# One tile shape for the products of attention and a long convolution on one core: eight tiles of 64 rows and 32 columns into two banks, one score tile a turn

## The chip, the cores and the metric

The kernel runs on one core of a Trainium2 chip, as one program. The metric is device microseconds from start to end, lower is better. Times of the kernel before are given from three runs, and one further execution was profiled; the profile's lines are of that execution.

## The reference

Two computations that share nothing but the output, whose halves they fill:

```python
def _A_ref(x, wq, wk, wv, wo):           # x: 1 x 2048 x 512, 32 heads of 16, one shared k and v
    q = (x @ wq).reshape(B, S, H, Dh).transpose(0, 2, 1, 3)
    k = x @ wk
    v = x @ wv
    p = softmax(einsum("bhqd,bkd->bhqk", q, k) * (Dh ** -0.5))
    o = einsum("bhqk,bkd->bhqd", p, v)
    return o.transpose(0, 2, 1, 3).reshape(B, S, H * Dh) @ wo

def _B_ref(q, k, v, shift_k, ssm_k, ssm_D):   # 1 x 2048 x 512
    # k_shift: causal convolution of 4 taps along S, per channel
    kv = k_shift * v
    y = irfft(rfft(kv, 2 * S) * rfft(ssm_k, 2 * S))[:S]   # causal convolution over all of S, per channel
    return q * (y + kv * ssm_D)

out = concatenate([_A_ref(...), _B_ref(...)], axis=-1)
```

## The kernel before

**Attention.** The 2048 queries of 32 heads form 32 groups of 4 heads times 512 queries (`NQ` = 32), and the keys 16 blocks of 128 (`NKT` = 16). A *score tile* is one key block for two heads, 128 keys by 2 x 512 queries; there are 2 x 32 x 16 = 1024 of them. For each, `scores` (L784) makes two matmuls side by side, one head in array rows 0 to 48 and one in rows 64 to 112 (each number split into f16 parts, 49 rows with the shift), into the two PSUM banks of a buffer `s`; ScalarE takes the exponential of both banks at once into a buffer `p` (L792). `pv` (L821, for the last group L806) then multiplies `p` by `vx` (v and a column of ones, 32 columns, f32) and adds over the key blocks into a sum: four column tiles of 128 rows by 32 columns side by side, 256 columns a step, one step for each score tile. After 32 steps VectorE copies the sum to `ao` (L831), and SyncE stores it.

**The other work** is cut into generators, called threads: the query projections (`rest_of_q`), the division of finished heads (`wo_heads`), the output projection (`wo_part`), and the convolution as a transform of 2048 = 128 x 16 points: matmuls with tables for the 128 (`forward`, `backward`), VectorE for the 16 (`dft4`, `dft16`, `product`) and the short convolution (`conv_short`). Their matmuls go through `mm` (L203): four column tiles of 128 rows by 32 columns. Transposes (L305) and the bounds of the queries (L638) have other shapes.

**The order** is written out by the program itself, and each engine works its own instructions strictly in this order. `attend` makes turns of three score tiles: three times `scores`, then `pv` steps, and around them what `_Fill` hands out of the threads. `_Fill` holds a credit of TensorE units and one of VectorE nanoseconds; both grow each turn by `RATE`, up to `MOST`. A thread yields what its next piece costs; `WHOLE` pieces are made at once, `PARTS` may be split. `hurry` puts a thread first when its due step comes near.

**PSUM** has eight banks: three score buffers of two banks (`ps`), and two single banks (`pf`), which the sum of `pv` and the products of the threads share in turn. SBUF holds seven buffers `p` (`PB`).

Of the kernel before, what the change touches and what calls it, by code (L numbers as in the profile page):

```python
# [19 lines left out]
P = 128  # L20
# [7 lines left out]
KR = 49  # L28
# [19 lines left out]

RATE = 3.0, 2500.0
EASY = 2  # L50
MOST = 4.0, 2900.0
# [41 lines left out]
WHOLE, PARTS = 0, 1  # L93


class _Emit:
    def __init__(self, ctx, tc, I, out):
        self.ctx, self.tc, self.nc, self.I, self.out = ctx, tc, tc.nc, I, out
        e = ctx.enter_context
        self.c = e(tc.tile_pool(name="c", bufs=1))  # L100
        self.ps = e(tc.tile_pool(name="ps", bufs=3, space=PSUM))
        self.pf = e(tc.tile_pool(name="pf", bufs=2, space=PSUM))
        self.w = e(tc.tile_pool(name="w", bufs=2))
        self.dr = e(tc.tile_pool(name="dr", bufs=1, space=DRAM))
        self.n = 0
        self.step = 0
        self.seen = set()

# [4 lines left out]
    def bank(self):  # L113
        return self.pf.tile([P, 512], F32, tag="f", name=self.nm("f"))
# [90 lines left out]
    def columns(self, bank, first, w, x, last=False, dve=0):  # L205

        n, k = 0, x.shape[-1] // P
        while n < k:  # L210
            g = yield k - n, dve, CONT if bank else NEW, PARTS
            start = not bank
            if start:
                bank.append(self.bank())
            c = slice(P * n, P * (n + g))
            n += g
            self.mm(bank[0][:, P * first + c.start : P * first + c.stop], w, x[:, c], start, last and n == k)
# [5 lines left out]
    def products(self, bank, pairs, last=False, dve=0):  # L223

        n, k = 0, len(pairs)
        while n < k:
            g = yield k - n, dve, CONT if bank else NEW, PARTS
            start = not bank
            if start:
                bank.append(self.bank())  # L230
            for w, x in pairs[n : n + g]:
                n += 1
                self.mm(bank[0], w, x, start, last and n == k)
                start = False
# [15 lines left out]
    def forward(self, src, c, m, ft):  # L250

        b = []
        for q in range(2):
            yield from self.columns(b, 2 * q, ft[:, q, :], src, q == 1, 700 * q)
        self.nc.vector.tensor_copy(c[:, :, m, :], b[0].rearrange("p (q n) -> p q n", q=2))  # L255
# [9 lines left out]
    def conv_load(self):  # L265
# [6 lines left out]
        yield 1, 600, NEW, WHOLE  # L272
        tp = self.bank()
        for ct in range(4):
            nc.tensor.transpose(tp[0:4, ct * P : (ct + 1) * P], sk[:, ct, :], self.ident)
        tps = w.tile([4, 512], F32, tag="s2", bufs=S2, name="tps")
        nc.vector.tensor_copy(tps, tp[0:4, :])
# [14 lines left out]
    def long_forward(self, blk, hin, ch):  # L292
# [8 lines left out]
        def turn(m):  # L301
            b = self.bank()
            for i in range(2):
                for ct in range(2):
                    nc.tensor.transpose(b[:, (2 * i + ct) * P : (2 * i + ct + 1) * P], hv[:, ct, m + i], self.ident)  # L305
            hT[m] = self.s2("hT")
            nc.vector.tensor_copy(hT[m], b.rearrange("p (i n) -> p i n", i=2))

        for m in (0, 2):
            yield 2, 700, NEW, WHOLE  # L310
            turn(m)
        for m in range(0, 16, 2):
            if m < 12:
                ft[m // 2 + 2] = self.table("ff", m // 2 + 2)
                yield 2, 700, NEW, WHOLE
                turn(m + 4)
# [80 lines left out]
    def backward(self, blk, cx, places):  # L397
# [15 lines left out]
        for m2 in range(8):  # L413
# [5 lines left out]
            b = []  # L419
            for i in range(2):  # L420
                m = 2 * m2 + i
                for cc in range(2):
                    x = cx[:, cc, 4 * g2[m // 4] + g1[m % 4], :]
                    last = i == cc == 1
                    yield from self.columns(b, 2 * i, ft[m2][:, i, cc, :], x, last, 700 * last)
            nc.vector.tensor_tensor(r, b[0].rearrange("p (i n) -> p i n", i=2), q[m2], ALU.mult)  # L426
# [93 lines left out]
    def x_turn(self, c):  # L520

        nc = self.nc
        b = [self.wide() for _ in range(2)]
# [18 lines left out]
    def kv(self):  # L542

        b = self.bank()
# [36 lines left out]
    def v_turn(self, kv):  # L581

        nc = self.nc
        b = self.bank()
# [6 lines left out]
    def k_max(self, kv):  # L591
# [6 lines left out]
        b = self.bank()  # L598
# [16 lines left out]
    def q_out(self, g, c, b, spread=False):  # L615
# [3 lines left out]
        nc.vector.tensor_scalar(cut, b, LIM, -LIM, ALU.min, ALU.max)  # L619
# [33 lines left out]
    def prologue(self):  # L653
# [15 lines left out]
        b = self.bank()  # L669
# [3 lines left out]
        self.x_turn(1)  # L673
        for dk in range(4):
# [10 lines left out]
        b = self.bank()  # L685
        cut = [self.k_cut(0, rows[0])]
        self.bound(0, 0, b, st)
        b1 = self.bank()
# [13 lines left out]
        self.scores(2)  # L702
# [8 lines left out]
    def rest_of_q(self):  # L711
# [5 lines left out]
        for c in range(4):  # L717
            for g in range(4):
# [3 lines left out]
                if c or g > 1:  # L722
                    b = []
                    for dk in range(4):
                        pairs = self.three(self.wq[g][:, :, dk, :], self.xT[c][:, :, dk, :])
                        yield from self.products(b, pairs, dk == 3, 2600 * (dk == 3))
                    self.q_out(g, c, b[0])
                yield WAIT, 2
                yield 2, 1100, NEW, WHOLE
                self.bound(g, c, self.bank())  # L730
# [21 lines left out]
    def flag(self):  # L752
# [10 lines left out]
        yield 1, 200, NEW, WHOLE  # L763
        b = self.bank()
# [5 lines left out]
    def scores(self, u):  # L770
# [11 lines left out]
        for e in range(2):  # L782
            rows = slice(64 * e, 64 * e + KR)
            self.nc.tensor.matmul(  # L784
                s[:, e, :],
                self.kst[rows, k * P : (k + 1) * P],
                part(rows),
                start=True,
                stop=True,
            )  # L790
# [4 lines left out]
    def pv(self, x):  # L795

# [4 lines left out]
        if n == NQ - 1:  # L801
            h, k = divmod(x % (2 * NKT), NKT)
            if k == 0:
                self.acc = self.bank()
            for j in range(4):
                nc.tensor.matmul(  # L806
                    self.acc[32 * j : 32 * j + 32, 0:256],
                    self.vx[:, k, :],
# [431 lines left out]
```

## Time and profile before

| | us |
|---|---|
| three runs | 1046.73 (median), 1045.3 to 1048.16 |
| the profiled execution | 1045.31 |
| its span | 1043.5 |
| VectorE's copies of sums (31) | 21.4 |
| DMA, mean over the span | 84 GB/s |
| granted TensorE clock, mean | 0.996 |

The span runs from the first to the last instruction in the profile; the execution's time has a little around it. A group of the profile gives a line, an engine, an operation and tiles, then the count, the busy time, the mean duration of one in ns, and the idle time of the engine just before them with what ended it. A matmul's duration holds the way through the array, so several overlap: the distance between starts says what one costs in a row of them. PEld is TensorE's loading of weights, which runs beside matmuls. An f32 matmul stands in the profile as two instructions with one weight load each; in the lists of the order below it is one row, and its loads aren't shown. A timeline's row gives start, length and a count of like instructions that follow each other, and in brackets the idle time ahead with its cause.

### The profile page before, as it was taken

The numbers are of one execution on the slowest core, as the hardware profiler recorded it, in microseconds if no ns is written. First come the engines' busy times: TensorE is split into PE (matmuls) and PEld (weight loads), VectorE is DVE, ScalarE is ACT, GpSimd is POOL, SyncE is SP. The second block draws the span as 40 slices with busy tenths as digits, with TensorE's granted clock in tenths as the row PEclk, the third lists the DMA queues.
The fourth block names the chain that finished last, engine by engine and source line by source line (L and its number), as shares of the span: only waits on it lengthen the run. The fifth ranks groups of instructions, "written<-read, shape, count | busy, mean of one in ns | idle before, by whom it ended". The sixth has DMA issues, their size and how long they took to land.

```text
span 1043.5 us, 31945 instructions
## 1 busy us (share of the span) xinstructions
PE 990.4 (95%) x14019; PEld 449.3 (43%) x14019; DVE 654.4 (63%) x881; ACT 972.4 (93%) x1039; POOL 105.0 (10%) x158
## 2 busy tenths in 40 slices
PE   6899999999999999999999999999999899999986
PEld 4344444444433334444444444444444334444432
DVE  4736873877497887776861578378888990211133
ACT  4699989999999999999999999999999999999994
POOL 4131301000000000030101312000000000121000
PEclk9999999999999999999999999999999999999999
DMA  7335524112211211031314534101032101331101
GB/s 243 128 97 181 190 77 167 45 51 82 91 56 45 75 35 40 22 122 57 96 56 132 183 123 149 42 20 44 33 97 71 52 29 40 109 121 45 51 2 44
DMA packets 47549, 87.30 MB, mean 84 GB/s; under 512 B 11132, under 2 KB 26026, under 8 KB 46380
## 3 DMA queue, kind: packets, MB, share of 16 engines
q1 hardware_dynamic: 33996, 43.50, 12.9%
q0 software_dynamic: 11648, 40.89, 12.1%
q8 instruction: 111, 1.82, 0.7%
q10 hardware_dynamic: 1760, 0.81, 0.3%
q14 instruction: 34, 0.28, 0.1%
HBM read 60.16 MB, written 25.02 MB: 82 GB/s over the span
## 4 chain that ended last, share of the span: by engine, by line
PE 70%; ACT 15%; DVE 8%; issue 6%; DMA 1%; ACTq 0%; SPq 0%
PE f L821 32%; PE s L784 22%; ACT p L792 14%; PE f L203 14%; DVE sp L141 2%; DVE ao L831 1%; PE f L305 1%; PE f L806 1%; DMA wqf<-in_A_wq 1%; DVE xT L540 1%; PE x L203 0%; ACT xT L539 0%; DVE sp L395 0%; DVE sp L255 0%; DVE t L362 0%
## 5 line engine op out<-in xcount | busy, mean ns | idle before, releaser
L792 ACT ACTIVATE p<-s 128x1024 f32<-128x1024 f32 x1024 | 960.1, 1037 | 41.5 <-PE s L784 35.9
L821 PE MATMUL f<-p,vx 128*32 128x256 f32 x7936 | 494.7, 381 | 8.1 <-DVE ao L831 8.1
L784 PE MATMUL s<-st,kst 49*128 49x512 f16 x2048 | 317.6, 380 | 19.1 <-ACT p L792 16.4
L821 PEld LDWEIGHTS f<-p,vx 128*32 128x32 f32 x7936 | 235.1, 110 | 196.9 <-issue 33.6
L784 PEld LDWEIGHTS <-kst 49*128 49x128 f16 x2048 | 100.1, 94 | 253.3 <-issue 206.5
L141 DVE TENSOR_TENSOR sp<-sp 128x1024 f32<-128x1024 f32 x96 | 111.5, 1213 | 0.0
L255 DVE COPY sp<-f 128x512 f32<-128x512 f32 x64 | 44.1, 689 | 63.6 <-PE f L203 62.5
L831 DVE COPY ao<-f 128x512 f32<-128x512 f32 x31 | 21.4, 691 | 71.4 <-PE f L821 71.4
L203 PE MATMUL f<-xT,wq 128*32 128x512 f16 x768 | 58.8, 391 | 0.1
L141 DVE TENSOR_TENSOR sp<-sp,sp 128x1024 f32<-128x1024 f32 x48 | 56.3, 1216 | 0.2
L203 PE MATMUL f<-wo,o 128*32 128x512 f16 x720 | 54.4, 383 | 0.0
L426 DVE TENSOR_TENSOR r<-f,q 128x512 f32<-128x512 f32 x16 | 11.0, 688 | 63.0 <-PE f L203 63.0
L259 POOL DMA_DIRECT2D ff<-in_ff x32 | 17.5, 548 | 266.7 <-PE f L203 266.7
L203 PE MATMUL f<-a,ff 128*32 128x256 f32 (+1 forms) x648 | 38.8, 338 | 1.6 <-DVE sp L255 1.6
L203 PE MATMUL f<-hT,ff 128*32 128x256 f32 (+1 forms) x648 | 38.8, 338 | 0.0
L203 PE MATMUL f<-sp,fi 128*32 128x256 f32 (+1 forms) x680 | 38.3, 331 | 0.0
L427 POOL DMA_DIRECT2D out<-r x16 | 11.5, 717 | 250.1 <-DVE rl L879 147.0
L364 DVE TENSOR_TENSOR a<-a,t 128x512 f32<-128x512 f32 x48 | 33.2, 691 | 1.5
L362 DVE TENSOR_TENSOR t<-kk,tpb 128x512 f32<-128x512 f32 x48 | 32.7, 681 | 0.0
L934 DVE TENSOR_SCALAR wp<-f 128x512 f32<-128x512 f32 x12 | 8.3, 690 | 38.8 <-PE f L203 38.8
L619 DVE TENSOR_SCALAR cut<-f 128x512 f32<-128x512 f32 x16 | 11.0, 689 | 32.3 <-PE f L203 32.2
L203 PEld LDWEIGHTS f<-a,ff 128*32 128x32 f32 x648 | 18.0, 109 | 17.2 <-issue 6.3
(141 smaller groups left out, 602.6 us busy)
## 6 DMA issues: line engine op xcount, KB each, us to landing
ff<-in_ff POOLq DMA_DIRECT2D x32, 256.0 KB, 5.0
od<-ao SPq DMA_DIRECT2D x30, 256.0 KB
kk<-in_B_k POOLq DMA_DIRECT2D x12, 640.0 KB, 4.9
qd<-qp SPq DMA_DIRECT2D x48, 128.0 KB
st<-qd SPq DMA_DIRECT2D x60, 98.0 KB
v<-in_B_v POOLq DMA_DIRECT2D x16, 256.0 KB, 4.8
hin<-in_B_ssm_k POOLq DMA_DIRECT2D x4, 1024.0 KB, 6.8
fi<-in_fi POOLq DMA_DIRECT2D x16, 256.0 KB, 3.8
```

The source lines that it names most:

```text
L141: v.tensor_tensor(part(out), part(a), part(b), op)
L203: self.nc.tensor.matmul(out[j : j + 32], w[:, j : j + 32], x, start=start, stop=stop)
L255: self.nc.vector.tensor_copy(c[:, :, m, :], b[0].rearrange("p (q n) -> p q n", q=2))
L259: self.nc.gpsimd.dma_start(t, self.I[n][:, 2 * m2 : 2 * m2 + 2])
L362: nc.vector.tensor_tensor(t, kx(i), tap(i), ALU.mult)
L364: nc.vector.tensor_tensor(a, a, t, ALU.add)
L426: nc.vector.tensor_tensor(r, b[0].rearrange("p (i n) -> p i n", i=2), q[m2], ALU.mult)
L427: nc.gpsimd.dma_start(self.orr[:, 2 * m2 : 2 * m2 + 2, D + blk * CB : D + (blk + 1) * CB], r)
L784: self.nc.tensor.matmul(s[:, e, :], self.kst[rows, k * P : (k + 1) * P], part(rows), start=True, stop=True,)
L792: self.nc.scalar.activation(p, s, AF.Exp, scale=DH**-0.5 / SC / SC)
L821: nc.tensor.matmul(self.acc[32 * j : 32 * j + 32, cols], self.vx[:, k, :], self.pt[2 * i + j // 2][:, j % 2, cols], start=k == h == 0, sto ...
L831: nc.vector.tensor_copy(a, self.acc)
```

## The change

Every product after the prologue is made by eight tiles at once, four of 32 columns in each half of the array's rows (rows 0 to 63 and 64 to 127), and the two halves write different PSUM banks. What was one matmul over 128 rows becomes two over 64.

- `scores` (now L803): eight matmuls of 49 rows by 32 columns for a tile, in place of two by 128 columns.
- `pv` (now L847): eight matmuls of 64 rows; the halves' sums lie in two banks, and after the 32 steps VectorE copies one (L857) and adds the other (L858). In the second half of the last group the old form with 128 rows stays (L829).
- The threads' products: `job` (L235) takes the place of `columns` and splitted `products`. It makes two results (or two halves of one) in two banks, in two passes: in the first, rows 0 to 63 go to bank 0 and rows 64 to 127 to bank 1, in the second the other way round. The second pass comes at the earliest three turns after the first.
- PSUM: two score buffers of two banks (`ps`), one pair of banks for the products (`pf`), and one for the sums (`pa`).
- A turn of `attend` is one score tile: `scores(u)`, then `pv(u - 3)` (`LAG`), then at most one piece of TensorE work from the threads. When a sum is complete, two turns go without `pv`, and the next two make two steps each, with no other work. A thread's next product may start two turns after a job has ended.
- The credits are per tile: 1.05 units and 850 ns, up to 2.0 and 1500.
- In the prologue the second and fourth turn of x, the first query products and some small ones use `pf` and `pa`, and the third score tile moves into the loop.

The diff, cut to what matters:

```diff
-RATE = 3.0, 2500.0
-EASY = 2
-MOST = 4.0, 2900.0
+RATE = 1.05, 850.0
+EASY = 1.5
+BESIDE = 2.0, 2.0, 0.0
+MOST = 2.0, 1500.0
+LAG = 3
...
-        self.ps = e(tc.tile_pool(name="ps", bufs=3, space=PSUM))
-        self.pf = e(tc.tile_pool(name="pf", bufs=2, space=PSUM))
+        self.ps = e(tc.tile_pool(name="ps", bufs=2, space=PSUM))
+        self.pf = e(tc.tile_pool(name="pf", bufs=1, space=PSUM))
+        self.pa = e(tc.tile_pool(name="pa", bufs=1, space=PSUM))
...
+    def job(self, entries, dve):
...
+        for t in range(2):
+            left = list(entries)
+            while left:
+                most = yield left[0][1], dve, NEW if t == 0 and len(left) == len(entries) else CONT, at
...
+                while left and self.spent + left[0][1] <= most:
+                    cols, unit, *wx = left.pop(0)
+                    self.spent += unit
+                    for j in range(0, P, 32):
+                        for e in range(2):
+                            k = e ^ t
+                            rows = slice(64 * e, 64 * e + 64)
+                            self.nc.tensor.matmul(
+                                b[j : j + 32, k, cols],
+                                wx[2 * k][rows, j : j + 32],
+                                wx[2 * k + 1][rows],
...
+            at = self.u + 3
...
     def x_turn(self, c):
...
-        b = [self.wide() for _ in range(2)]
+        b = [self.bank(), self.sums()] if c % 2 else [self.wide() for _ in range(2)]
...
     def scores(self, u):
...
-        for e in range(2):
-            rows = slice(64 * e, 64 * e + KR)
-            self.nc.tensor.matmul(
-                s[:, e, :],
-                self.kst[rows, k * P : (k + 1) * P],
+        for j in range(0, P, 32):
+            for e in range(2):
+                rows = slice(64 * e, 64 * e + KR)
+                m = self.nc.tensor.matmul(
+                    s[j : j + 32, e, :],
+                    self.kst[rows, k * P + j : k * P + j + 32],
...
     def pv(self, x):
...
         for j in range(4):
-            nc.tensor.matmul(
-                self.acc[32 * j : 32 * j + 32, cols],
-                self.vx[:, k, :],
-                self.pt[2 * i + j // 2][:, j % 2, cols],
+            for e in range(2):
+                rows = slice(64 * e, 64 * e + 64)
+                nc.tensor.matmul(
+                    self.acc[32 * j : 32 * j + 32, e, cols],
+                    self.vx[rows, k, :],
+                    self.pt[2 * i + j // 2][rows, j % 2, cols],
...
-        nc.vector.tensor_copy(a, self.acc)
+        nc.vector.tensor_copy(a, self.acc[:, 0, :])
+        nc.vector.tensor_tensor(a, a, self.acc[:, 1, :], ALU.add)
...
     def attend(self, fill):
...
-        for u in range(3, 2 * steps + 3, 3):
-            for t in range(u, min(u + 3, 2 * steps)):
+        for u in range(2, tiles + 2):
+            t = u
+            if t < tiles:
...
+            done = 0
+            while done < 2 and x <= u - LAG and rest <= 0:
+                self.pv(x)
+                x += 1
+                done += 1
+                if x in full:
+                    rest = 3
+            rest -= 1
+            fill.turn(u, self.step, BESIDE[done] if u > LAG else 0)
```

What this does to the order is seen on TensorE. Before, a turn in the middle of the query projections (`wq` into `f`), with `s`, `st` and `kst` of the scores and `p`, `vx` of the p·v steps; each load and matmul of scores and products stands once, for the repeated ones left out:

```order
L784 LDWEIGHTS kst
L784 MATMUL s_4662<-st_3989,kst 128x512
...
L784 MATMUL s_4667<-st_3989,kst 128x512
...
L784 MATMUL s_4672<-st_4435,kst 128x512
L203 LDWEIGHTS wq_90
L203 MATMUL f_4615<-xT_1953,wq_90 32x512
...
L821 MATMUL f_4352<-p_4601,vx 32x256 x2
L821 MATMUL f_4352<-p_4628,vx 32x256 x2
...
L821 MATMUL f_4352<-p_4633,vx 32x256 x2
L821 MATMUL f_4352<-p_4638,vx 32x256 x2
```

The shape changes twice in three tiles: behind the scores, and ahead of the next turn's. On TensorE in the changed kernel, two turns in the same work:

```order
L803 LDWEIGHTS kst
L803 MATMUL s_9654<-st_8976,kst 32x512
...
L847 MATMUL acc_8722<-p_9502,vx 32x256 x4
L847 MATMUL acc_8722<-p_9549,vx 32x256 x4
L235 LDWEIGHTS wq_93
L235 MATMUL f_9515<-xT_2171,wq_93 32x256
...
L803 MATMUL s_9690<-st_8976,kst 32x512
...
L847 MATMUL acc_8722<-p_9592,vx 32x256 x4
L847 MATMUL acc_8722<-p_9628,vx 32x256 x4
```

Each score tile's matmuls now stand ahead of one p·v step and a piece of product, all in tiles of 32 columns. And on TensorE at the end of a group of 32 tiles, where the sum `acc` changes:

```order
L847 MATMUL acc_13642<-p_14295,vx 32x256 x4
L847 MATMUL acc_13642<-p_14314,vx 32x256 x4
L235 MATMUL f_14360<-hT_13710,ff_13629 32x128 x16
...
L803 MATMUL s_14419<-st_13805,kst 32x512
...
L803 MATMUL s_14430<-st_13805,kst 32x512
...
L803 MATMUL s_14441<-st_13805,kst 32x512
...
L847 MATMUL acc_14452<-p_14333,vx 32x256 x4
L847 MATMUL acc_14452<-p_14370,vx 32x256 x4
```

Two score tiles pass with no p·v step between them, and the first step of the new sum stands behind the third one's scores.

More of the change, by code (lines that the diff above doesn't have):

```diff
@@ L219, in three, with whole, products @@
+    def whole(self, units, dve):
+        yield units, dve, NEW
+        self.spent = units
+        return self.bank()
     def three(self, w, x):
         return [(w[:, i], x[:, j]) for i, j in ((0, 0), (1, 0), (0, 1))]
[L223 to L234, printed above, removed]
+    def products(self, pairs):
+        h = [slice(0, 256), slice(256, 512)]
+        return [(h[0], 0.5, w, x[:, h[0]], w, x[:, h[1]]) for w, x in pairs]
@@ L250, in forward @@
     def forward(self, src, c, m, ft):
[L252 to L255, printed above, removed]
+        h = [slice(0, P), slice(P, CB)]
+        b = yield from self.job([(x, 1, ft[:, 0, :], src[:, x], ft[:, 1, :], src[:, x]) for x in h], 700)
+        self.nc.vector.tensor_copy(c[:, :, m, :], b[:, :, 0:CB])
     def table(self, n, m2):
@@ L618, in q_out @@
         cut = w.tile([P, 512], F32, tag="s2", bufs=S2, name=self.nm("cut"))
-        nc.vector.tensor_scalar(cut, b, LIM, -LIM, ALU.min, ALU.max)
+        nc.vector.tensor_scalar(cut if len(b.shape) == 2 else self.two(cut), b, LIM, -LIM, ALU.min, ALU.max)
         qp = w.tile([P, 2, 512], F16, tag="s2", bufs=S2, name=self.nm("qp"))
@@ L673, in prologue @@
         self.x_turn(1)
+        b = self.bank()[:, 0, :]
         for dk in range(4):
```

253 lines of the change are left out of this document (125 added, 128 removed).

## The prediction

> **What bounds the kernel now.** I read the page first (busy times, then the chain), then the groups by line, then the timeline of the attention loop, and last the waits. In the page, the busy line shows two engines close to the span, and the chain line shows which of them the end hangs on:
>
> ```profile
> PE 990.4 (95%) x14019; PEld 449.3 (43%) x14019; DVE 654.4 (63%) x881; ACT 972.4 (93%) x1039; POOL 105.0 (10%) x158
> PE 70%; ACT 15%; DVE 8%; issue 6%; DMA 1%; ACTq 0%; SPq 0%
> L792 ACT ACTIVATE p<-s 128x1024 f32<-128x1024 f32 x1024 | 960.1, 1037 | 41.5 <-PE s L784 35.9
> L821 PE MATMUL f<-p,vx 128*32 128x256 f32 x7936 | 494.7, 381 | 8.1 <-DVE ao L831 8.1
> L784 PE MATMUL s<-st,kst 49*128 49x512 f16 x2048 | 317.6, 380 | 19.1 <-ACT p L792 16.4
> ```
>
> ScalarE does one exponential for each of 1024 score tiles and waits for TensorE's scores; TensorE rarely waits for it. Both are nearly full, so the loop's price must be taken apart engine by engine. ScalarE's own floor comes from its rows by line 792 (durations min/median/max, first and last start) and from a stretch of its timeline in which three exponentials run without a gap:
>
> ```profile
> L792 ACT ACTIVATE p<-s x1024: 1015/1027/1294, 33.3 to 1026.2; 128x1024 f32<-128x1024 f32 x171
> 874.68 2.85 ACT L792 ACTIVATE p<-s 128x1024 f32<-128x1024 f32 x3 [0.39 <-PE s L784]
> ```
>
> Three take 2.85 us and the last one 1.03 of it, so one starts 0.91 us after another: (2.85 - 1.03) / 2. At that pace 1023 steps take 931 us. They took 1026.2 - 33.3 = 993 us. So **62 us of the loop are ScalarE waiting**, mostly in gaps too short for the 41.5 us of idle that the group's row counts. Before the first exponential lie 33.3 us, after the start of the last one 1043.5 - 1026.2 = 17.3 us, and the profiled execution took 1045.31 us, 1.8 more than its span. With no wait at all the kernel would take 33.3 + 931 + 17.3 + 1.8 = **983 us**.
>
> TensorE's side is read from one turn of three score tiles in the timeline (start, length, rows), and from two rows that hold a single shape or a single wait:
>
> ```profile
> 500.18 0.82 PE L784 MATMUL s<-st,kst 49*128 49x512 f16 x6
> 500.94 0.86 PE L203 MATMUL f<-sp,fi 128*32 128x256 f32 x16
> 501.61 1.48 PE L821 MATMUL f<-p,vx 128*32 128x256 f32 x24
> 503.02 0.95 PE L784 MATMUL s<-st,kst 49*128 49x512 f16 x6
> 12.55 2.77 PE L203 MATMUL f<-xT,wq 128*32 128x512 f16 x48
> L203 PE MATMUL f<-xT,wq 128*32 128x512 f16 x768 | 58.8, 391 | 0.1
> ```
>
> The row from 12.55 is twelve groups of four column tiles, and one matmul of them lasts 0.39 by its group: (2.77 - 0.39) / 11 = 0.216 us for 512 columns in f16. Six groups of L821 (three p·v steps, each 256 columns in f32 as two rows a tile) should then stream in 6 x 0.216 = 1.30 us, but scores start 1.41 us behind them; three score tiles should take 0.65, but the products start 0.76 behind. Between L203 and L821, which share one shape, the 0.67 us is the 0.65 of the streams. So each change between the score shape (two tiles of 64 rows, 128 columns) and the others (128 rows, 32 columns) costs about 0.11 us. Some 341 turns with two changes make about 75 us of TensorE. This is what the change goes for.
>
> **The change, part by part.** (1) *One shape.* Scores become eight matmuls of 64 x 32, p·v and the products eight of 64 x 32 into two banks. Streaming time stays if eight tiles run at once: counting matmuls in the changed order, scores 8192 / 8 x 0.216 = 221 us, p·v with the last group's 442, f16 products 5568 / 8 x 0.108 = 75, f32 products 3072 / 8 x 0.216 = 83, and 37 turns with work in another shape about 18: together **839 us**, 0.82 a tile against ScalarE's 0.91. No row shows eight tiles at once. The near bounds are the score rows (two row tiles into two banks in one 0.216) and the products' four column tiles: at no cost, 0.216 a group. From the other end, if the two row halves took turns, p·v and products would double, which adds 600 us; the score rows, with two halves at once, lie much nearer the first, and I take 0.216 with up to 10% on it.
>
> ```profile
> 1018.09 0.16 PEld L203 LDWEIGHTS f<-wl,lr 128*32 128x32 f32 x8 [0.42 <-issue]
> L203 PEld LDWEIGHTS f<-sp,fi 128*32 128x32 f32 x680 | 17.8, 109 | 14.7 <-issue 8.6
> ```
>
> Weight loads double, but eight of 0.11 us lie within 0.16, some 7 ns apart, and run beside the streams; cover fails only if a pair costs over 0.108 / 8 = 13 ns in the densest f16 group. I cost them at nothing.
>
> (2) *A turn is one tile, with two score buffers in place of three.* The wait for a score buffer now stands in every turn, and behind it on TensorE's queue stand p·v and the products. Its price is a round trip:
>
> ```profile
> 35.91 10.19 ACT L792 ACTIVATE p<-s 128x1024 f32<-128x1024 f32 x11 [0.65 <-PE s L784]
> 36.98 0.39 PE L784 MATMUL s<-st,kst 49*128 49x512 f16 x2 [0.69 <-ACT p L792]
> 1017.34 0.82 PE L784 MATMUL s<-st,kst 49*128 49x512 f16 x6
> 1017.83 9.36 ACT L792 ACTIVATE p<-s 128x1024 f32<-128x1024 f32 x10 [2.19 <-PE s L784]
> ```
>
> An exponential from 35.91 lasts 1.03 and frees its buffer; the scores start at 36.98, 0.04 later. From scores to the exponential they release are 1017.83 - 1017.34 = 0.49, and 0.03 more for eight starts. So 1.03 + 0.04 + 0.52 = 1.59 us, against two exponentials, 1.82: TensorE may be **0.23 us late** before ScalarE waits. In the order, 386 turns hold 0.65 us of streams, 205 hold 0.86, 95 hold 0.97 and about 230 hold 1.08. A 1.08 turn (two units of products) makes TensorE 0.17 late, and the lighter turns behind it give that back: inside the 0.23. Two places overrun. At the 31 group ends two turns of double p·v (1.08 each) follow two without: 0.34 late, 0.11 lost, up to 0.28 where a full turn follows; some 6 us. The 16 turns with transposes change shape:
>
> ```profile
> L305 PE MATMUL f<-ident,hin 128*128 128x128 f32 x64 | 11.4, 301 | 0.9 <-DVE sp L255 0.9
> ```
>
> 11.4 / 16 = 0.71 us each, with 0.65 of the turn's own about 1.4 with a change: 0.25 over, 4 us. I take 12 us in all; ends: 5 (light turns absorb more), and 50 if every group streams 10% longer, since then the 0.23 is used up in most filled turns.
>
> (3) *One buffer for sums, one for products.* The sum is now copied by two VectorE instructions (copy, add), and the next p·v may not start before both; the order leaves two turns without p·v for it. The product buffer is reused two turns after a job. Behind a late VectorE stands all of TensorE, scores included.
>
> ```profile
> L141 DVE TENSOR_TENSOR sp<-sp 128x1024 f32<-128x1024 f32 x96 | 111.5, 1213 | 0.0
> L831 DVE COPY ao<-f 128x512 f32<-128x512 f32 x31 | 21.4, 691 | 71.4 <-PE f L821 71.4
> PE f L821 <- DVE ao L831: 8.1, 19, 1.2
> ```
>
> Before, this wait came 19 times, 8.1 us on TensorE's matmuls, at most 1.2. Giving VectorE's rows in the changed order their durations (0.69 for 512 columns, 1.21 for 1024), two pieces of 64 tiles hold 0.95 and 0.98 us a tile, over ScalarE's 0.91, and four others 0.86 to 0.91. The overflow alone is (0.04 + 0.07) x 64 = 7 us; 17 of the 31 copies have more than 1.6 us of VectorE rows ahead or of their own. I take **15 us**, between 5 (the overflow, partly absorbed) and 35 (an average 0.8 us at each of the 17 copies, and as much again before product jobs). The 31 added adds, 31 x 0.69 = 21 us of VectorE, are in these rows.
>
> (4) *Prologue and end.* The first query product now waits for a buffer that the second turn of x uses:
>
> ```profile
> 13.27 2.36 DVE L540 SCALAR_TENSOR_TENSOR xT<-x,xT 128x1024 f16<-128x1024 f32 x2 [1.11 <-ACT xT L539]
> ```
>
> The first of these two ends near 14.45, where the product (the 12.55 row above) started at 12.55: 1.9 us later; but the fourth turn of x no longer queues for a score buffer, which gives most of it back. I take +1 (0 to 2). The end keeps its steps: 0 (-2 to +2).
>
> Sum, against the profiled execution of 1045.31: 983 + 12 + 15 + 1 = **1011 us**. The median of the runs, 1046.73, is 1.4 above that execution; nothing is added for it.
>
> **The rivals.** *A: buffers take the place of the shape changes.* VectorE's ends and the 0.23 us run out together: 35 for VectorE, 20 for long turns, 983 + 55 + 1 = 1039, between 1033 and 1050. For it: VectorE's two overfull pieces; against it: the 8.1 us of such waits before.
>
> *B: slower, by the start of matmuls.* The fastest steady rate that the rows show is the 128-column group, four tiles in half of 0.216 us, 27 ns a matmul. One such group in the timeline, and the mean of one matmul of it:
>
> ```profile
> 503.90 0.32 PE L203 MATMUL f<-sp,fi 128*32 128x128 f32 x4
> L203 PE MATMUL f<-sp,fi 128*32 128x128 f32 x336 | 17.3, 278 | 0.0
> ```
>
> If no matmul could follow another sooner than that, scores (8 x 27 = 216) and p·v (16 x 27 = 432) would still fit, but every product would take twice its streams: 839 + 158 = 997 us of TensorE. Filled turns grow to 1.5 us, six times the slack, and the light ones cannot give it back. TensorE alone gives 33.3 + 997 + 17.3 + 1.8 = 1049, with the unevenness **1090** (1050 to 1125). It decides from about 18 ns: there products take 4/3 as long, filled turns 1.3 us. Against it: starts within a group lie 14 ns apart or less (the 503.90 row: four of 0.278 us in 0.32) and loads 7. The Trainium skill (TensorE: Matmul & The Clock Gate, "Wait — 56ns, not 53.3ns?") states a floor of about 25 ns from one matmul's start to the next; by it products would take 293 us in place of 158, an estimate of 974 us of TensorE and some 1080 in all. The 503.90 row undercuts that floor for tiles in different columns; no row here shows it for eight.
>
> *C: the shape still changes.* If 49 rows after 64, or f16 after f32, emptied the array as the shapes do now, each one-tile turn would pay twice 0.11: 1022 x 0.22 = 225 us on 821, so 33.3 + 1046 + 17.3 + 1.8 = 1098. Against it: L203 to L821 above pay nothing, and here f16 products run into f32:
>
> ```profile
> 291.46 0.61 PE L203 MATMUL f<-xT,wq 128*32 128x512 f16 x8
> 291.90 0.39 PE L821 MATMUL f<-p,vx 128*32 128x256 f32 x4
> ```
>
> Two groups, 0.43, and L821 starts 0.44 behind them.
>
> **How the numbers follow.** Forecast 0.75 (985 to 1033: the terms at their low ends to 983 + 50 for long turns); A 0.08; B 0.12; C 0.05. The prediction is 1011. The range, 985 to 1050, takes in the forecast and A and leaves B and C out, 0.17, and a little below 985. About 0.3%, 3 us, is what a measurement can tell from no change: faster than 1043.6 are the forecast and three quarters of A, 0.81; within it 0.03; slower 0.16.
>
> **What would show it.** Right: scores, p·v and products following each other at 0.216 a group with no 0.11 at a change; ScalarE's starts mostly 0.91 apart; its remaining waits at group ends, transposes and behind VectorE's copies. Wrong: matmul starts 20 ns or more apart within a group of eight; TensorE still in the chain for most of the span; waits of p·v on line 858, or of products on VectorE's copies, above 35 us; a first exponential later than 36 us.

## The result, and the profile after

The changed kernel takes **1183.83 us** (median of 4 runs, 1182.08 to 1190.15) against 1047.45 (1045.3 to 1049.25, 4 runs) for the kernel before on the same chip: a ratio of **1.131, with an interval from 1.127 to 1.135**. It was forecast at 1011 us and came out slower. The profiled execution took 1190.15 us, 1.8 more than its span.

The page after: the span, the busy line, the queue that carries instructions (packets, MB, share of the DMA engines), the chain by engine, and the groups that carry the attention loop:

```profile
span 1188.4 us, 77103 instructions
...
PE 1022.1 (86%) x36579; PEld 703.4 (59%) x36579; DVE 676.9 (57%) x913; ACT 985.9 (83%) x1039; POOL 105.1 (9%) x158
...
q8 instruction: 288, 4.72, 1.7%
...
PE 59%; ACT 17%; issue 12%; DVE 4%; DMA 1%; ACTq 0%; DVEq 0%
...
L811 ACT ACTIVATE p<-s 128x1024 f32<-128x1024 f32 x1024 | 973.7, 1034 | 168.1 <-PE s L803 162.3
L847 PE MATMUL acc<-p,vx 64*32 64x256 f32 x15872 | 729.7, 381 | 38.9 <-issue 36.5
L803 PE MATMUL s<-st,kst 49*32 49x512 f16 x8192 | 533.9, 384 | 49.5 <-issue 22.2
```

The reader is to see three things. ScalarE is busy as long as before (973.7 against 960.1 us) but now waits 162 us for scores, where it waited 36. TensorE has 36,579 matmuls and as many weight loads, 73,158 instructions where it had 28,038. And the instruction queue moved 288 packets; the same row of the kernel before reads

```profile
q8 instruction: 111, 1.82, 0.7%
```

A packet is 4.72 MB / 288 = 16.4 KB, and 288 x 256 = 73,728: each packet is a block of 256 TensorE instructions (before: 111 x 256 = 28,416).

The sum by the prediction's own terms starts from the view of ScalarE's line (durations min/median/max, first and last start):

```profile
L811 ACT ACTIVATE p<-s x1024: 1009/1026/1243, 37.2 to 1170.0; 128x1024 f32<-128x1024 f32 x171
```

The first exponential starts at 37.2 us (33.3 before), the 1023 steps to the last one take 1170.0 - 37.2 = 1132.8 us, of which 931 are ScalarE's floor at 0.91 and **202 are waiting** (62 before, 27 forecast), and 18.4 us follow. So the whole loss is in the loop, and is waiting for scores.

First, what the change promised does happen. A stretch of TensorE's timeline without a stop (start, length, rows):

```profile
433.18 0.41 PE L803 MATMUL s<-st,kst 49*32 49x512 f16 x8
433.39 0.63 PE L847 MATMUL acc<-p,vx 64*32 64x256 f32 x16
433.82 0.52 PE L235 MATMUL f<-xT,wq 64*32 64x256 f16 x24
434.15 0.41 PE L803 MATMUL s<-st,kst 49*32 49x512 f16 x8
434.37 0.63 PE L847 MATMUL acc<-p,vx 64*32 64x256 f32 x16
```

Scores start 0.21 ahead of p·v, p·v 0.43 ahead of the products, three half-width groups of products 0.33 ahead of the next scores: eight tiles do run at once at 0.216 a group, and the 0.11 us at a change of shape is gone. This turn took 0.97 us, its streams and nothing else.

What is new is in another stretch. TensorE's timeline there:

```profile
109.81 0.32 PE L235 MATMUL f<-a,ff 64*32 64x128 f32 x5
109.88 0.41 PE L803 MATMUL s<-st,kst 49*32 49x512 f16 x2
113.90 0.61 PE L803 MATMUL s<-st,kst 49*32 49x512 f16 x4 [3.61 <-issue]
```

ScalarE's timeline over the same time:

```profile
108.69 1.94 ACT L811 ACTIVATE p<-s 128x1024 f32<-128x1024 f32 x2 [0.49 <-PE s L803]
114.63 1.03 ACT L811 ACTIVATE p<-s 128x1024 f32<-128x1024 f32 x1 [3.99 <-PE s L803]
```

And the DMA queues' view, cut to 111.45 to 112.5 us (packets, MB, share):

```profile
q8 instruction: 1, 0.02, 5.5%
```

TensorE stops in the middle of eight score matmuls of one tile, waits for nothing that the program asked for ("issue"), and goes on 4 us later; ScalarE loses the same 4 us. The packet of instructions is the event between: by its record it landed at 112.43, and TensorE resumed 1.47 us after. Counting TensorE's records in order, 142 of its gaps over 0.45 us from start to start stand at one place in a count modulo 256. (The place moves by one or two at a time along the trace, by the few records that the profile lacks.) These are the *block-end gaps*; together they are 123 us longer than a normal step, and the kernel before has no such row of gaps. Mostly TensorE resumes 1.2 to 1.5 us after a block's packet has ended. Of the 202 us, 141 lie in exponentials that came late behind such a gap. The view of waits (us in total, times, longest) names the same thing under "issue":

```profile
PEld L803 <- issue: 169.6, 345, 4.0
ACT p L811 <- PE s L803: 162.3, 210, 8.0
PEld acc L847 <- issue: 72.2, 100, 3.1
...
PE f L235 <- issue: 45.1, 52, 2.8
...
PE s L803 <- ACT p L811: 16.7, 38, 1.0
...
PEld acc L847 <- DVE ao L858: 1.2, 3, 0.5
```

TensorE's wait for VectorE's second instruction on a sum (the add in line 858), which the prediction feared, is 1.2 us.

### The profile page after: what moved, and what is told of

Read it like the earlier page. It is cut to its first block, busy times and chain, and to the rows that moved or that the text cites. A ratio compares the mean times of both kernels' runs of the same rounds, so it can differ in the third digit from the quotient of the medians.

```text
span 1188.4 us, 77103 instructions
## 1 busy us (share of the span) xinstructions
PE 1022.1 (86%) x36579; PEld 703.4 (59%) x36579; DVE 676.9 (57%) x913; ACT 985.9 (83%) x1039; POOL 105.1 (9%) x158
## 3 DMA queue, kind: packets, MB, share of 16 engines
q8 instruction: 288, 4.72, 1.7%
## 4 chain that ended last, share of the span: by engine, by line
PE 59%; ACT 17%; issue 12%; DVE 4%; DMA 1%; ACTq 0%; DVEq 0%
PE acc L847 27%; ACT p L811 17%; PE s L803 17%; PE f L235 13%; PE acc L829 1%; PE f L327 1%; DVE sp L146 1%; DMA v<-in_B_v 1%; PE f L208 0%; DVE ao L857 0%; DVE sp L415 0%; DVE qa L649 0%; DVE ao L858 0%; DVE cut L639 0%; PE f L658 0%
## 5 line engine op out<-in xcount | busy, mean ns | idle before, releaser
L811 ACT ACTIVATE p<-s 128x1024 f32<-128x1024 f32 x1024 | 973.7, 1034 | 168.1 <-PE s L803 162.3
L847 PE MATMUL acc<-p,vx 64*32 64x256 f32 x15872 | 729.7, 381 | 38.9 <-issue 36.5
L803 PE MATMUL s<-st,kst 49*32 49x512 f16 x8192 | 533.9, 384 | 49.5 <-issue 22.2
L847 PEld LDWEIGHTS acc<-p,vx 64*32 64x32 f32 x15872 | 381.6, 107 | 121.9 <-issue 72.2
L803 PEld LDWEIGHTS <-kst 49*32 49x32 f16 x8192 | 211.8, 91 | 192.6 <-issue 169.6
L235 PE MATMUL f<-wo,o 64*32 64x256 f16 x2880 | 96.3, 271 | 6.5 <-issue 6.5
L235 PE MATMUL f<-xT,wq 64*32 64x256 f16 x2688 | 83.0, 270 | 14.9 <-issue 13.9
L235 PE MATMUL f<-sp,fi 64*32 64x128 f32 x2048 | 65.5, 275 | 15.4 <-issue 14.4
L235 PEld LDWEIGHTS <-o 64*32 64x32 f16 x2880 | 64.9, 92 | 21.4 <-issue 10.9
L235 PEld LDWEIGHTS <-wq 64*32 64x32 f16 x2688 | 55.5, 91 | 33.2 <-issue 19.5
L235 PEld LDWEIGHTS f<-sp,fi 64*32 64x32 f32 x2048 | 49.0, 107 | 25.2 <-issue 17.8
L235 PE MATMUL f<-a,ff 64*32 64x128 f32 x2048 | 55.8, 271 | 8.0 <-issue 6.7
L235 PE MATMUL f<-hT,ff 64*32 64x128 f32 x2048 | 51.3, 272 | 4.7 <-issue 3.7
L235 PEld LDWEIGHTS f<-a,ff 64*32 64x32 f32 x2048 | 42.6, 105 | 18.7 <-issue 12.0
L857 DVE COPY ao<-acc 128x512 f32<-128x512 f32 x31 | 21.3, 689 | 49.6 <-PE acc L847 49.6
L235 PEld LDWEIGHTS f<-hT,ff 64*32 64x32 f32 x2048 | 39.4, 105 | 14.9 <-issue 6.0
```

What stands on the lines that cost most here:

```text
L235: self.nc.tensor.matmul(b[j : j + 32, k, cols], wx[2 * k][rows, j : j + 32], wx[2 * k + 1][rows], start=t == 0 and len(left) == len(entrie ...
L803: m = self.nc.tensor.matmul(s[j : j + 32, e, :], self.kst[rows, k * P + j : k * P + j + 32], part(rows), start=True, stop=True,)
L811: self.nc.scalar.activation(p, s, AF.Exp, scale=DH**-0.5 / SC / SC)
L847: nc.tensor.matmul(self.acc[32 * j : 32 * j + 32, e, cols], self.vx[rows, k, :], self.pt[2 * i + j // 2][rows, j % 2, cols], start=k == h ...
L857: nc.vector.tensor_copy(a, self.acc[:, 0, :])
```

## The experiments

**Theory 1 (code):** TensorE's instructions arrive in blocks of 256, one round trip at a time, and the changed kernel uses them faster than they come. **Rivals:** one buffer for sums and products; a cost of each start, load or dispatch on TensorE itself; the rows of the array in use. "Late" below is the time from the first to the last exponential's start over 931 us. Block-end gaps are counted as above, and instructions are matmuls and loads by the page. Half_pv, narrow_pv, wide_f32, wide_tiny, half_all, stream and old_scores are single runs; the others are medians of four or more.

| kernel | TensorE instructions | time, us | late, us | block-end gaps |
|---|---|---|---|---|
| before | 28,038 | 1047 | 62 | none |
| wide_pv | 45,574 | 1060 | 77 | 4 |
| half_pv | 57,286 | 1076 | 90 | 18 (18 us) |
| wide_all | 61,446 | 1067 | 84 | 24 (28 us) |
| wide_f32 | 67,014 | 1115 | 127 | 83 (67 us) |
| changed | 73,158 | 1184 | 202 | 142 (123 us) |
| wide_tiny | 77,318 | 1231 | 248 | 200 (147 us) |
| narrow_pv | 104,902 | 1612 | 625 | 369 (516 us) |

The runs half_all, old_scores and stream stand outside the table: in the first the clock changes, in the second the tile shape, and the third is another program.

**half_pv** leaves out the products of keys 64 to 127 of each tile in p·v, and with them half of p·v's instructions (all groups but the last):

```
-            for e in range(2):
+            for e in range(1):
...
-        nc.vector.tensor_tensor(a, a, self.acc[:, 1, :], ALU.add)
+        nc.vector.tensor_tensor(a, a, self.acc[:, 0, :], ALU.add)
```

> Leaves out the matmuls of rows 64 to 127 in p.v (all groups but the last; VectorE adds the first bank twice), so TensorE has 57,560 instructions in place of 73,432, with the same streams on the time axis, the same shape, turns, buffers and VectorE work. Code theory (TensorE gets its instructions in blocks of 256, and two blocks never come sooner than about 3.4 us after one another): 225 blocks in place of 287, most gaps at the ends of blocks go, 1030 to 1070 us. Buffer theory (two score buffers, one sum, one product buffer, VectorE late): same as the changed kernel, 1170 to 1195. Dispatch theory (17 ns for a pair of load and matmul): 28 pairs a turn in place of 35, 1140 to 1180.

Measured 1075.88 us, a little above the range. Block-end gaps fell from 142 to 18, with VectorE's copies and both buffers as they were. But the run has a trouble of its own, seen by windows (busy time of each engine, granted clock, DMA share, GB/s):

```profile
100.00:800.00 700.00, 661.66 (x20180) 444.81 (x20174) 508.43 (x660) 669.06 (x720) 61.57 (x96) 0.99 0.25 82
800.00:900.00 100.00, 95.98 (x2067) 55.13 (x2056) 73.69 (x95) 83.59 (x88) 1.98 (x3) 0.73 0.16 49
```

For 100 us the granted clock was 0.73 in place of 0.99, and 88 exponentials ran in that time, where the 700 us ahead of it hold 720, or 103 in each 100 us. The direction is as code says; the size is not clean.

**narrow_pv** does the same p·v work in twice as many matmuls, 128 columns each:

```
-        cols = slice(256 * h, 256 * h + 256)
...
+        for c, j, e in ((c, j, e) for c in range(2) for j in range(4) for e in range(2)):
+                part = slice(256 * h + 128 * c, 256 * h + 128 * c + 128)
```

> The same work, with each p.v matmul of 256 columns cut into two of 128: 105,176 TensorE instructions, the same streams. Code theory: 411 blocks at 3.5 us or more, 1440 to 1560 us. Buffer theory: unchanged, 1170 to 1200. Dispatch theory: 51 pairs a turn at 17 ns are 0.87 us on the average and 1.2 in filled turns, 1220 to 1300.

Measured 1612.12 us: beyond what code foretold, and out of reach of the rivals' numbers. Two rows of its page:

```profile
q8 instruction: 412, 6.75, 1.7%
...
L811 ACT ACTIVATE p<-s 128x1024 f32<-128x1024 f32 x1024 | 998.4, 1024 | 566.1 <-PE s L803 550.8
```

No sum and no buffer was added, yet 428 us came with 31,744 instructions, 124 blocks more: 3.45 us a block.

**wide_f32** goes the other way, with all work kept: the convolution's products take 256 columns in one matmul in place of twice 128.

```
-        h = [slice(0, P), slice(P, CB)]
-        b = yield from self.job([(x, 1, ft[:, 0, :], src[:, x], ft[:, 1, :], src[:, x]) for x in h], 700)
+        x = slice(0, CB)
+        b = yield from self.job([(x, 2, ft[:, 0, :], src[:, x], ft[:, 1, :], src[:, x])], 700)
...
-                for x in (slice(0, P), slice(P, CB)):
+                for x in (slice(0, CB),):
```

> The same work, with the convolution's matmuls over 256 columns in place of two of 128: 67,288 instructions, and the filled turns fall from 112 instructions to 80 in the same 1.08 us. Code theory: 263 blocks, and a block of filled turns lasts 3.5 us in place of 2.5, 1100 to 1150 us. Buffer theory: 1170 to 1200, as before.

Measured 1114.62 us, in code's range: 24 blocks fewer, 69 us less, though the columns that stream are the same.

**half_all** leaves out rows 64 to 127 in p·v and in all products of the loop, to look at half the rows with few instructions:

```
-                        for e in range(2):
+                        for e in range(1):
...
-            for e in range(2):
+            for e in range(1):
```

> Leaves out rows 64 to 127 in p.v and in all products of the threads (each pass writes one bank from rows 0 to 63): 45,848 instructions, the same streams, turns, buffers and VectorE rows. Code theory: 179 blocks, no gap at their ends any more; what is left over 983 us is the price of the buffers and the long turns, which the prediction put at 27: 1000 to 1030. Buffer theory: 1170 to 1195.

Measured 1711.69 us, which no theory had. The page (busy line, and the granted clock in tenths over 40 slices) shows why it says nothing of code:

```profile
PE 1675.0 (98%) x22787; PEld 913.6 (53%) x22787; DVE 677.9 (40%) x913; ACT 1053.0 (62%) x1039; POOL 104.8 (6%) x158
...
PEclk9555555555555555555555555555555555555559
```

The granted clock was half through the loop, and one score matmul lasted 611 ns on the mean where it had lasted 384. There was no gap at a block end.

**stream** measures the disputed cost alone: TensorE with nothing beside it.

`eight(…, columns, n)` makes n times eight matmuls, one in each tile of 64 rows by 32 columns:

```
+    eight(nc, b, x, x, 512, 256)
+    eight(nc, b, x, x, 256, 512)
+    eight(nc, b, x, x, 128, 512)
+    eight(nc, b, x, x, 64, 512)
+    for _ in range(256):
+        for j in range(0, P, 32):
+            nc.tensor.matmul(b[j : j + 32, 0, :], x[:, j : j + 32], x, start=True, stop=True)
```

> This kernel measures the disputed cost by itself and computes nothing of the reference: TensorE alone runs, one after the other, 2048 matmuls of 64 rows by 32 columns with 512 columns of f16 moving, 4096 with 256, 4096 with 128, 4096 with 64 (eight tiles at a time), and then 1024 of 128 rows by 32 columns with 512. Theory 1 (TensorE's instructions are fetched in blocks of 256 with a round trip of 3.3 to 3.4 us, so no more than about 75 load and matmul instructions start in a us, however short they are): the matmuls with 512 columns run at their work, about 55 us (75 instructions in a us, just at the limit); those with 256, 128 and 64 columns all take the same, 105 to 115 us each, with a gap at every 256th instruction; the last part 55 us without gaps. Theory 2 (no such limit; a load and its matmul cost what their columns cost, with a floor of 3.4 ns at a start): 55, 55, 27 and 14 us, then 55. Theory 3 (a load and its matmul take 16.6 ns of TensorE's own time, as pairs did in a queue that had been empty): 55, 68, 68 and 68 us, evenly, without gaps at the 256th.

The groups by line, shapes apart (busy time, mean ns of one, idle time before them):

```profile
L21 PE MATMUL b<-x 64*32 64x256 f16 x4096 | 65.1, 277 | 51.8 <-issue 51.7
L21 PE MATMUL b<-x 64*32 64x512 f16 x2064 | 61.4, 394 | 12.3 <-issue 7.0 <-DVE x L31 4.1 <-DVE y L42 0.8
...
L21 PE MATMUL b<-x 64*32 64x128 f16 x4096 | 60.2, 303 | 57.5 <-issue 57.5
L40 PE MATMUL b<-x 128*32 128x512 f16 x1024 | 57.2, 387 | 0.0
L21 PE MATMUL b<-x 64*32 64x64 f16 x4096 | 41.0, 230 | 76.4 <-issue 76.4
```

4096 matmuls take 65.1 + 51.8 = **116.9 us with 256 columns, 117.7 with 128 and 117.4 with 64**: a quarter of the columns changes nothing. That is a little over the 105 to 115 us that theory 1 gave. The time belongs to the 8192 instructions, 70 in a us. The large tiles of the last group (four at a time, 2048 instructions) do the same streaming as the first 2048 matmuls, in 57.2 us with no wait at all. TensorE's timeline shows how it goes:

```profile
104.32 1.94 PE L21 MATMUL b<-x 64*32 64x256 f16 x128 [1.79 <-issue]
108.04 1.94 PE L21 MATMUL b<-x 64*32 64x256 f16 x128 [1.79 <-issue]
111.50 1.94 PE L21 MATMUL b<-x 64*32 64x256 f16 x128 [1.51 <-issue]
...
419.26 1.28 PE L21 MATMUL b<-x 64*32 64x64 f16 x128 [2.20 <-issue]
422.73 0.44 PE L21 MATMUL b<-x 64*32 64x64 f16 x33 [2.19 <-issue]
```

A block of 128 loads and 128 matmuls runs at full pace and is used up, then TensorE waits; blocks start 3.5 or 3.7 us apart, some 4.0, whatever is in them. The last full block also settles rival B of the prediction: 128 matmuls with 64 columns start within 1.28 - 0.23 = 1.05 us, **8 ns apart**, far under the 27 ns that would have been needed. Theory 3's even 68 us a part is not there.

**wide_all** adds to wide_f32 that the f16 products take 512 columns, two results of a projection at once, one in each bank (the planner's rates are 1.1 units and 900 ns a turn and its EASY 2, so that the same work is done by the last scores):

```
-            pairs += self.three(self.oc[G][:, :, i * P : (i + 1) * P], self.wo[G % 4])
-        b = yield from self.job(self.products(pairs), 700)
...
+            a, b = (self.three(self.oc[G][:, :, k * P : (k + 1) * P], self.wo[G % 4]) for k in (i, i + 1))
+            entries += [(slice(0, 512), 1, *p, *q) for p, q in zip(a, b)]
```

> The convolution's products with 256 columns in one matmul, and the f16 products with 512: two results of a projection are worked out at once, one in each bank, in place of two halves of one result. The same sums, 61,720 TensorE instructions in place of 73,432 (the kernel before has 28,312). The planner's rate is 1.1 units a turn and up to two f16 entries go in a turn, so that the same work is done when the last scores run. Theory 1 (code fetch): the fullest turns of the loop have 80 instructions in 1.08 us in place of 112, a block of 256 lasts 3.4 us, so most gaps at block ends go; 1040 to 1070 us. Rival (buffers of the wider jobs and VectorE): each job now holds the one product buffer twice as long in the f16 part, so waits on VectorE grow; 1150 to 1200 us. Rival (shape, dispatch or density of rows): the work in each turn is the same as in the changed kernel; 1114 us as with the wide f32 products alone, or more.

Measured 1066.56 us, a ratio to the kernel before of 1.016 (1.012 to 1.021): in code's range, 117 us under the changed kernel with the same work and buffers that are held longer, not shorter. Its page, the chain by engine and ScalarE's group:

```profile
ACT 43%; PE 28%; DVE 15%; issue 12%; DMA 1%; ACTq 0%
...
L821 ACT ACTIVATE p<-s 128x1024 f32<-128x1024 f32 x1024 | 955.6, 1063 | 67.3 <-PE s L813 63.5
```

ScalarE is now the largest part of the chain, as the prediction had wanted it.

**wide_tiny** is wide_all with instructions added that do next to nothing:

```
+        if n < NQ - 1:
...
+                    self.nc.tensor.matmul(s[j : j + 32, e, 0:1], self.kst[rows, k * P + j : k * P + j + 32], part(rows)[:, 0:1], start=True, stop=True)
```

> The kernel of wide_all, with one thing added: before the eight matmuls of a turn's scores, eight more with the same weights and a single column, into places that the scores then overwrite (not in the last unit). 77,592 TensorE instructions in place of 61,720, with next to no work in the added ones. Theory 1 (code fetch): 76 instructions a turn on the mean and 96 in the fullest, over the limit of about 71 in 0.95 us; 1130 to 1200 us, with some 150 gaps at block ends or more. Rival (TensorE's time alone): the eight pairs cost 0.03 to 0.06 us in a turn that has 0.07 us free on the mean, so within 20 us of wide_all, and no more gaps at block ends than there.

Measured 1231.47 us, 165 more, above even code's range. Two rows of its page:

```profile
q8 instruction: 304, 4.98, 1.7%
...
L826 ACT ACTIVATE p<-s 128x1024 f32<-128x1024 f32 x1024 | 980.2, 1029 | 207.3 <-PE s L818 197.3
```

62 blocks more than wide_all (242), and block-end gaps went from 24 to 200; of the 163 us by which exponentials came later, 148 lie behind such gaps. With wide_all this is the pair that shows the cause: instructions taken away without work, and put back with next to none. The higher planner's rates of wide_all, which are a second change there, stand in both.

**wide_pv** takes p·v with 512 columns every second turn, on top of wide_all:

```
+        if h == 0:
+            return
...
-        cols = slice(256 * h, 256 * h + 256)
+        cols = slice(0, 512)
```

> wide_all, and in p·v one matmul with 512 columns in every second turn in place of one with 256 columns in each: the same sums and the same eight tiles, 45,848 TensorE instructions in place of 61,720. Theory 1 (code fetch): 45 instructions a turn on the mean, 80 in the fullest turn (now 1.51 us) and 128 in any pair of turns (1.9 us), below what arrives; of wide_all's 85 us in exps that came late, the 28.5 at block ends go and part of the 23 in which TensorE was behind by its own pace: 1010 to 1045 us, so no slower than the kernel before. Rival (eight tiles of 64 rows with two banks of their own are slow in themselves, or the two buffers of scores and the one of products bind): nothing in this is changed, and the turns become uneven (0.65 and 1.51 us), so 1066 us or more.

Measured 1059.64 us, a ratio of 1.012 (1.010 to 1.014). The four block-end gaps left make 3 us of late exponentials, but code's number was missed: the time fell by 7 us, not by 20 or more. The rival's 1066 or more was missed too, by 6 us. TensorE's timeline in one place:

```profile
607.10 1.05 PE L859 MATMUL acc<-p,vx 64*32 64x512 f32 x16
607.96 0.41 PE L813 MATMUL s<-st,kst 49*32 49x512 f16 x8
608.17 1.05 PE L859 MATMUL acc<-p,vx 64*32 64x512 f32 x16
609.03 0.41 PE L813 MATMUL s<-st,kst 49*32 49x512 f16 x8
613.27 1.11 PE L235 MATMUL f<-a,ff 64*32 64x256 f32 x16 [3.82 <-DMA ff<-in_ff]
```

What is late now has other causes. Giving each matmul of this trace its price by columns (0.216 us for eight with 512 in f16) and each exponential 0.91, with two score buffers and nothing else, 42 of the 77 us come out of the uneven turns alone; the same sum for the changed kernel's order gives 10, for wide_all's 13. The other 35 are waits such as the one at 609 for a table that a transfer brings, and those of the view of waits below. None of them was taken away by itself, so this split is worked out, not shown.

```profile
PEld f L235 <- DVE sp L278: 11.9, 28, 1.8
PEld f L327 <- DVE sp L278: 5.7, 7, 1.5
PEld L235 <- DVE gm L675: 5.2, 6, 1.6
```

**old_scores** puts the score shape of the kernel before into wide_pv:

```
-        for j in range(0, P, 32):
-            for e in range(2):
...
+        for e in range(2):
+            rows = slice(64 * e, 64 * e + KR)
+            self.nc.tensor.matmul(s[:, e, :], self.kst[rows, k * P : (k + 1) * P], part(rows), start=True, stop=True)
```

> wide_pv, with the scores as the kernel before has them: two matmuls of 64 rows by 128 columns a turn in place of eight of 64 by 32. 33,560 TensorE instructions. It asks what one shape is worth when the instructions no longer bind. Theory 1 with the price of a change of shape as the trace of before has it (0.11 us, two changes in a turn): TensorE's mean turn goes from 0.86 to 1.08 us, over an exp's 0.91, so 1110 to 1160 us. Rival (the changes of shape hide beside exp, and the fewer instructions win): 1010 to 1045 us, as wide_pv or less.

Measured 1157.54 us: 33,286 instructions, fewer than in any other variant of the changed kernel, no block-end gap, and 98 us slower than wide_pv. The chain by engine, from its page:

```profile
PE 75%; ACT 13%; issue 7%; DVE 3%; DMA 1%; POOL 0%; ACTq 0%; POOLq 0%
```

And a stretch of TensorE's timeline:

```profile
501.68 0.39 PE L812 MATMUL s<-st,kst 49*128 49x512 f16 x2
502.00 0.66 PE L235 MATMUL f<-hT,ff 64*32 64x256 f32 x16
502.60 0.39 PE L812 MATMUL s<-st,kst 49*128 49x512 f16 x2
```

Scores of 0.216 take 0.32 until the products start, and products of 0.43 take 0.60: the change of shape costs 0.10 us behind the scores and 0.17 ahead of them in each turn. So with turns of one tile and few instructions, one shape is worth the 98 us. That the changed kernel had as much from it is not shown: no run puts the old scores into that kernel, and the kernel before changed shape only twice in three tiles.

No version of these beats the kernel before; wide_pv, the best, is 124 us under the changed kernel and 12 over the one before.

## Why the prediction was wrong, point by point

- **Term 1, one shape: the streams were right, one step failed.** Eight tiles at 0.216 a group, no 0.11 at a change, and 839 us of streams (the records of the changed kernel, priced by columns, sum to 838.6) all held. The step that failed is "Weight loads double ... cover fails only if a pair costs over 0.108 / 8 = 13 ns in the densest f16 group. I cost them at nothing." It asked what a pair (a load and its matmul) costs TensorE when its instructions are there. Within a block pairs do start 8 ns apart (stream); over several blocks they came no faster there than about 70 instructions in a us, 28 ns a pair. The fullest turns hold 16 instructions for scores, 32 for p·v and 64 for two units of convolution: 112 in 1.08 us of streams, where 70 in a us makes 1.6. Even the mean was out of reach: the loop holds 72,475 recorded loads and matmuls, 283 blocks, which take 979 us at stream's shortest step of 3.46, against 931 + 27 = 958 us in the forecast. The prediction counted matmuls by what they stream, never instructions, though the page had the row for it: 111 packets of the instruction queue, which had to become about 288.
- **Size of that step.** 141 of the 202 late us stand directly behind block-end gaps; taking 11,712 instructions out with the same sums (wide_all, with the planner's rates raised) gave back 117 us of the time. The other 61 us of lateness are more than twice the 27 that terms 2 and 3 allowed. They were not split, so part of the miss, some 34 us, stays open.
- **Term 2, long turns (12 us):** the changed kernel's order, priced as above, gives 10. About right, as far as a sum without a run can say.
- **Term 3, VectorE and single buffers (15 us):** hardly visible in the changed kernel, where TensorE was late for another reason. Once code no longer binds, some 35 us remain in wide_pv beside the uneven turns, and the three rows of weight loads that wait for VectorE hold 23 us there. The upper end given was 35. Whether 15 was too small is not shown, since those 35 us hold other waits too, but the term is not the cause of the result.
- **Term 4, the prologue (+1):** the first exponential came at 37.2, 3.9 later than before, outside the 0 to 2 given and past the 36 that the prediction named as a sign of being wrong. The end grew by 1.1 us, inside its bounds.
- **The rivals.** A (buffers, 1039) did not happen here. B (a floor between starts, 1090) named the right engine and the wrong mechanism: its price is per start and stands in every group, while the traces show full pace inside a block and a stop at its end. The result, 1184, lies above its range too. The 25 ns of the Trainium skill (TensorE: Matmul & The Clock Gate, "Wait — 56ns, not 53.3ns?") does not hold for eight tiles: 8 ns in stream. C (the shape still changes) is refuted by the stretch from 433.18 us. What the range lacked was a case for the number of instructions.
- **A page spoke of it.** The Trainium skill (Runtime: NRT & Kernel Launch, "Instruction fetch mechanics") says that engines get instructions in blocks of 16 KiB, 256 instructions each, and that crossing a block's end is mostly hidden, as instructions issue more slowly than blocks arrive. The block agrees with the packets of 16.4 KB here. That it is hidden holds for the kernel before, with 28,038 instructions in 1043.5 us, and not at 73,158 in 1188.4.

## What to carry to other kernels

Before cutting matmuls into smaller tiles, count the loads and matmuls that result, per us in the densest stretch as well as in all, and set them against the rate at which the instruction queue brings blocks (here 256 in 3.5 to 4.0 us, about 70 in a us). Small tiles call for long moving operands: eight tiles of 512 f16 columns, 16 instructions in 0.216 us, already need 74 in a us, and 256 columns need twice that. In a trace the sign is a gap (here 0.5 to 4 us) with the releaser "issue", in the middle of a group, every 256 instructions, while the page's instruction packets have multiplied.

## What the runs showed of the hardware that was not expected

- Code arrived one block at a time, with a round trip of about 3.5 us. In the changed kernel's trace the medians of its parts are 1.15 us from TensorE's restart behind a block-end gap to the start of the next packet, 1.04 for the packet, and 1.38 from its landing to the next restart.
- A busy DMA goes with a late block. Ahead of the 4 us stop at 109.9 us no block's packet was moved from 105.9 to 111.5 us, while the DMA engines were 98% busy. Over all 142 block-end gaps, the next packet started a median of 1.14 us after the restart where other transfers filled less than a tenth of the DMA engines for the next 1.5 us (89 cases), and 2.5 us after it where they filled six tenths or more (14 cases). No run changed the transfers alone.
- The granted clock fell to half (0.52 over the run) when rows 64 to 127 of the array stood idle in p·v and the products, though TensorE was busy 98% of the time (half_all; the scores still used both halves). In stream it was 0.97 in the part with 256 columns and 0.51 and 0.50 in those with 128 and 64, and the time of a part was the same (116.9, 117.7 and 117.4 us): the arrival of code did not follow that clock. What decides the clock was not tried.
